# The first of eight experts on seven block products too, its normalisation moved into the units, and fill matmuls at the start of attention

## The chip, the cores and the metric

One core of a Trainium2 chip runs the whole program. The metric is device time in microseconds; lower is better. The engines are TensorE (matmul, PE), VectorE (DVE), ScalarE (ACT), GpSimd (POOL) and SyncE (SP, which issues most DMAs). All operands are float32. A float32 matmul is done here as three matmuls of `float32r` type: each factor is split into a high part (a rounded copy, on ScalarE) and a low part (the difference, on VectorE or GpSimd), and high x high, high x low and low x high are added up in PSUM.

## The reference

```python
attn_out = _attn_ref(q, k, v, proj)        # 2 x 8 heads, 768 positions, 64 wide; keys of another hash bucket are masked
x = attn_out.transpose(0, 2, 1, 3).reshape(1536, 512)
h = x @ w_in                               # 512 -> 2048
x = (h * tanh(softplus(h))) @ w_out        # Mish, 2048 -> 512
logits = x @ w_gate                        # 8 experts
P = exp(logits - logits.max())
for _ in range(8):
    P /= P.sum(1, keepdims=True) + 1e-09   # rows: one token's experts
    P /= P.sum(0, keepdims=True) + 1e-09   # columns: one expert's tokens
    P *= 1536 / 8
out = sum(P[:, e:e + 1] * (maximum(x @ w1[e], 0) @ w2[e]) for e in range(8))   # 512 -> 1024 -> 512
```

## The kernel before, in words

There are three stages. In each, every engine works through its own queue in the order in which the program issues to it.

**Attention** (`attention`, lines 178 to 772). Its steps are named tasks with engines, due times and predecessors. A planner written into the kernel (`COST`, `begin` and the loop below it) puts them in an order at build time, from costs in microseconds that stand in a table; a task's body is issued when it is chosen. `warm_up` (L268) is eight matmuls on zeros. For head h, `prep_hi` and `prep_lo` split q and k into high and low parts (head 0 in two halves, the others whole), `bits_mm` and `bits_cmp` make the bits of the hash, `s_mm` and `s_max` the row maxima, `st_mm`, `st_exp`, `split_hi`, `split_lo` and `av_mm` the rest. `clear` zeroes buffers on GpSimd once `proj_parts` (VectorE) is through. `decode` and `weight_hi`/`weight_lo` turn the first feed-forward weights, which come as 64-bit floats, into high and low parts.

**Feed-forward blocks** (lines 775 to 1098). The tokens are three blocks of 512 (`tb`), the hidden width is cut in chunks of 128 and the chunks in groups of four. `steps` lists (group, block, chunk): 48 steps for the Mish layer (chunks 0 to 15), then 24 for expert 0 (chunks 16 to 23, two groups). Loop n issues `up(n)` (12 matmuls into one PSUM bank, L814 to L816), `act(n)` (for Mish: ScalarE L826 and L827, VectorE L828) and `down(n - 3)` (12 matmuls into four banks, L850). After a block's last chunk `evacuate` adds the four banks to `acc` on VectorE (L863), and after the Mish layer `split` writes the high part `xh` on ScalarE (L866) and the low part `xl` on GpSimd (L867). What `at(n, f)` has put down is issued at the end of loop n. In this way the expert 0 steps carry beside them the `logits` of each block (8 matmuls, L876), eight whole rounds of `sinkhorn` (L904, VectorE), `spread` (four DMAs issued on ScalarE's queue, L922), and the eight token sums of the first token half, `make_t`: `raw_t` on VectorE (L975 to L981), a copy on ScalarE (L985) and the low part on VectorE (L986). They share the three scratch buffers of `t_p` with `act`.

**Units** (lines 1101 to 1297). Experts 1 to 7 take, for each half of the tokens (768) and each pair of hidden chunks, one unit. `product` computes the 2x2 block product with seven block products instead of eight (`PRODUCTS`, 42 matmuls of 384 columns, L1133), for which sums of token blocks (T1 to T4) and of weight blocks (S1 to S4, `unit_s` on GpSimd) are needed. The seven use two PSUM banks: 1, 3, 5 and 7 the one, 2, 4 and 6 the other, and `post` reads a bank between two of them. After product 1 ScalarE copies it to `p1` (L1160), product 3 is added into the same bank; after product 2 VectorE makes `u` from the other bank (L1153), product 4 is added into that. `rounded` and `rest` (L1141, L1146) split the hidden values, and `second` has the 36 matmuls of 512 columns with the second weight (L1200). `gather` adds the result, times `prob`, to `acc` (L1212). For the units to come, `unit_a`, `unit_s` and `unit_w` (ScalarE high, GpSimd low: L998, L1015 `s_lo`, L1022 `w_lo`) are issued by `job(u, s, f)` after product s, or after a quarter of the second products for s = 7 to 10. `scale_first` (L926) multiplies `acc` by expert 0's probability in units 0 to 3.

Of the kernel before, what the change touches and what calls it, by code (L numbers as in the profile page):

```python
# [16 lines left out]
P = 128  # L17
# [5 lines left out]
E = 8  # L23
# [16 lines left out]
WARM = 8  # L40
DELTA = 0.012
# [19 lines left out]
def lsh_attention_moe_kernel(  # L61
# [23 lines left out]
    cst = const.tile([P, 7 + 64], F32, name="cst")[:, 0:7]  # L85
# [13 lines left out]
    NW = N64 + NF  # L99
    NU = 2 * (E - 1) * NF // 2  # L100

    def unit(u):
        g, x = divmod(u, NU // 2)
        return g, 1 + x // (NF // 2), x % (NF // 2)
# [6 lines left out]
    def load_next():  # L111
# [9 lines left out]
        elif n < N64 + NW:  # L121
            t = stage_p.tile([P, 1024], F32, tag="stage", name="stage")
            nc.sync.dma_start(out=t, in_=w[n - 2 * N64])
            staged[n - N64] = t
        elif n < N64 + NW + 2 * NU:
            u, j = divmod(n - N64 - NW, 2)
# [34 lines left out]
    def source(i):  # L161
        return dec[i % NDEC] if i < N64 else staged[i]
# [5 lines left out]
    def convert_lo():  # L168
        i = converted[0]
        dst = ring[i % RING]  # L170
        nc.gpsimd.tensor_sub(dst[:, 1, :], source(i), f32(dst[:, 0, :]))
        converted[0] += 1
        if i >= N64:
            staged.pop(i)
            load_next()


    def attention():
        with ExitStack() as a:
# [36 lines left out]

            raw_t, hi_t, lo_t, psb_t, bit_t = {}, {}, {}, {}, {}
# [50 lines left out]
            def warm_up():  # L268
                t = ps_t.tile([P, 512], F32, tag="t", name="warm")
                for _ in range(WARM):  # L270
                    nc.tensor.matmul(t, xh[:, 0, 0:P], xh[:, 0, 0:512], start=True, stop=True)
# [8 lines left out]
            def count_rows(c):  # L280
# [3 lines left out]
                    scalar1=idt[96:100, 97:98], scalar2=float(S), op0=ALU.mult, op1=ALU.mult,  # L284
# [14 lines left out]
            def prep_lo(h, i, e):  # L299
                c = halves(h)[i]  # L300
# [27 lines left out]
            def bits_cmp(h, i):  # L328
                c = slice(i * HALF, (i + 1) * HALF)
                t = psb_t.pop(i)  # L330
                if h and i == 0:
                    bit_t[0] = bt_p.tile([44, S], F32R, tag="bit", name="bit")
                parts = [(bit_t[0], slice(0, 44))] if h else [(sq[0][64:76], slice(0, 12)), (bk[0][64:76], slice(32, 44))]
                for dst, r in parts[::-1 if i else 1]:
# [18 lines left out]
            def vsum_fin(h):  # L353
                hi, lo = (vs_p.tile([1, 2, D], F32R, tag=n, name=n) for n in ("vsh", "vsl"))
                m = vs_t[1][0:1, 0:P].rearrange("p (a d) -> p a d", a=2)
                nc.vector.tensor_copy(hi, m)
                nc.vector.tensor_sub(lo, m, f32(hi))
# [54 lines left out]
            def rows_cp(u):  # L412
# [7 lines left out]
                nc.scalar.activation(dst, src, AF.Identity, scale=cst[0:n, 5:6], bias=cst[0:n, 6:7])  # L420
# [97 lines left out]
            def task(engines, due, f, *args, after=(), cost=None, lag=0.01, ring=None, frees=None):  # L518
# [5 lines left out]
                    av_out=0.47, load_table=1.5, prep_hi=0.83, prep_move=0.83, rows_cp=0.25, st_exp=0.49,  # L524
# [4 lines left out]
                    prep_lo=0.96, s_max=0.95, cols=0.39, split_hi=0.31, split_v=0.35, vsum_red=1.53, vsum_fin=0.55,  # L529
# [3 lines left out]
                    clear=0.6, prep_lo=1.82, split_lo=1.0, split_v=0.73, norm=1.0, decode=1.3, weight_lo=2.35,  # L533
# [20 lines left out]
            task("A", -99, load_table, after=[nm(clear_start)])  # L554
            for j in range(4):
# [5 lines left out]
            for i in range(NS):  # L561
                for n, kind in enumerate(("sq", "bk", "one")):
                    e = "D" if (kind, i) in FAST else "P"
                    task(e, -8.5 + 3 * i + n / 4, clear, kind, i, after=[nm(clear, "bk", i)] * (n == 2) + [nm(proj_parts)] * (i > 0))
            for i in range(2):
                for kind in ("vt", "vh", "vl"):
                    task("P", -3 + 2 * i, clear, kind, i, after=[nm(proj_parts)])


            for h in range(NH):  # L570
# [6 lines left out]
                     after=[nm(prep_lo, hin, i) for i in range(len(halves(hin)))] if hin is not None else [])  # L577
                his = [nm(prep_hi, h, i) for i in range(len(halves(h)))]
                los = [nm(prep_lo, h, i) for i in range(len(halves(h)))]
                for i in range(len(halves(h))):  # L580
                    task("A", due - 14.0 if h else -50, prep_hi, h, i, cost=None if h else 0.45,
                         after=[nm(load_qk, h), *moved] + [nm(bits_mm, h - 1, j) for j in range(2) if h])
                    task("PD" if h else "D", due - 14.0 + 1 if h else -50, prep_lo, h, i, cost=None if h else 0.6, after=[his[i], *moved])
# [755 lines left out]
```

## Time and profile before

| | us |
|---|---|
| median of 3 runs (lowest, highest) | 1542.56 (1542.52, 1546.52) |
| the profiled execution's own time | 1542.95 |
| its span, first to last instruction | 1541.2 |
| TensorE matmul busy | 1523.3 (99%) |
| VectorE, ScalarE, GpSimd busy | 875.9, 681.3, 871.8 |

In a timeline or chain row the first number is the start in us from the span's beginning, the second the duration; "L850" is the line, "x12" means that many instructions in one row, and a bracket tells how long the engine was idle before and what ended that. Matmuls overlap in the pipeline, so two starts tell more than one duration. A VectorE or GpSimd duration includes time in which the started instruction is held up.

### The profile page before, as it was taken

Reading aid. Unit: us, or ns where it says so; the run is one execution under the profiler, and the core shown is the slowest. Engines: PE = TensorE matmul, PEld = TensorE weight load, DVE = VectorE, ACT = ScalarE, POOL = GpSimd, SP = SyncE. Lnnn points to the kernel's source line nnn. Section 1 sums busy time; section 2 is a strip of 40 time slices with the busy share of each in tenths; the row PEclk is TensorE's granted clock in tenths of the full one; section 3 lists DMA queues with packets and bytes.
Section 4 is the critical chain, followed back from the end, with each engine's and each line's share of the span. In section 5 each row is a group of like instructions: output and inputs, shape, how many; then the busy total and the mean of one; then the engine's idle time right before and its main releaser. Section 6 shows DMA issues by size and latency. Waiting matters only on the chain.

```text
span 1541.2 us, 20182 instructions
## 1 busy us (share of the span) xinstructions
PE 1523.3 (99%) x7396; PEld 1337.9 (87%) x7396; DVE 875.9 (57%) x1426; ACT 681.3 (44%) x1233; POOL 871.8 (57%) x715
## 2 busy tenths in 40 slices
PE   8999999999999999999999999999999999999999
PEld 6888888888888788889999898989898989899998
DVE  7889996746663228656444444676534444445353
ACT  5778777654443232233433333334433333333331
POOL 6887777333324230256666666666666666666661
PEclk9999999999999999999999999999999999999999
DMA  7745540122221010112222222222322222222211
GB/s 178 167 118 156 145 128 25 55 69 69 69 69 55 24 32 1 29 55 69 69 68 69 69 69 69 69 69 68 110 69 67 68 65 68 65 68 68 69 56 41
DMA packets 64387, 113.50 MB, mean 74 GB/s; under 512 B 19792, under 2 KB 20792, under 8 KB 64288
## 3 DMA queue, kind: packets, MB, share of 16 engines
q1 hardware_dynamic: 62688, 112.17, 25.1%
q8 instruction: 58, 0.95, 0.3%
q14 instruction: 41, 0.34, 0.1%
q10 hardware_dynamic: 1600, 0.05, 0.0%
HBM read 89.22 MB, written 3.15 MB: 60 GB/s over the span
## 4 chain that ended last, share of the span: by engine, by line
PE 90%; DVE 4%; DMA 2%; issue 2%; POOL 1%; ACT 1%; SPq 1%; DVEq 0%; ACTq 0%; POOLq 0%
PE y L1200 29%; PE u L1133 26%; PE y L850 13%; PE h L816 4%; PE h L814 4%; PE h L815 4%; PE pav L478 4%; PE ps L376 1%; PE pst L429 1%; PE pst L428 1%; DVE mx L390 1%; SPq L306 1%; DMA vt<-in_v_dram 1%; DMA sq<-row 0%; PE lg L876 0%
## 5 line engine op out<-in xcount | busy, mean ns | idle before, releaser
L1141 ACT ACTIVATE gh<-c 128x384 fp32r<-128x384 f32 x224 | 117.9, 526 | 153.4 <-DVE c L1153 151.6
L1153 DVE TENSOR_TENSOR u<-u,p 128x384 f32<-128x384 f32 x56 | 31.2, 558 | 266.8 <-PE u L1133 262.8
L1146 DVE SCALAR_TENSOR_TENSOR gl<-c,gh 128x384 fp32r<-128x384 f32 x224 | 168.2, 813 | 0.0
L1200 PE MATMUL y<-ww,gh 128*128 128x512 f32 x672 | 163.4, 391 | 0.0
L1200 PE MATMUL y<-w,gh 128*128 128x512 f32 x672 | 162.6, 391 | 0.0
L440 POOL TENSOR_TENSOR plo<-p,ph 128x384 fp32r<-128x384 f32 x128 | 137.3, 1084 | 43.2 <-ACT ph L437 29.5
L1200 PEld LDWEIGHTS y<-w,gh 128*128 128x128 f32 x672 | 125.7, 188 | 25.2
L1200 PEld LDWEIGHTS y<-ww,gh 128*128 128x128 f32 x672 | 125.7, 188 | 25.2
L152 POOL TENSOR_TENSOR stage<-stage,sgn 128x512 f32<-128x512 f32 x32 | 43.7, 1367 | 119.4 <-DVE sgn L150 112.1
L1022 POOL TENSOR_TENSOR w<-stage,w 128x1024 fp32r<-128x1024 f32 x28 | 66.8, 2386 | 78.4 <-ACT w L1018 78.4
L434 ACT ACTIVATE p<-pst 128x384 f32<-128x384 f32 x192 | 92.7, 486 | 40.0 <-PE pst L429 30.2
L850 PE MATMUL y<-gh,w 128*128 128x512 f32 x336 | 110.3, 389 | 0.0
L1022 POOL TENSOR_TENSOR ww<-stage,ww 128x1024 fp32r<-128x1024 f32 x28 | 66.9, 2390 | 74.3 <-ACT ww L1018 74.3
L1015 POOL TENSOR_TENSOR w<-sraw,w 128x1024 fp32r<-128x1024 f32 x28 | 68.3, 2440 | 67.7 <-ACT w L1011 67.7
L390 DVE TENSOR_REDUCE mx<-ps 128x1 f32<-128x768 f32 x95 | 90.2, 949 | 17.8 <-PE ps L376 17.1
L814 PE MATMUL h<-xh,w 128*128 128x512 f32 x252 | 98.4, 390 | 0.0
L816 PE MATMUL h<-xh,w 128*128 128x512 f32 x252 | 98.1, 389 | 0.1
L815 PE MATMUL h<-xl,w 128*128 128x512 f32 x252 | 98.1, 389 | 0.0
L998 POOL TENSOR_TENSOR wa<-stage,wa 128x512 fp32r<-128x512 f32 x28 | 40.3, 1438 | 97.2 <-ACT wa L993 69.5
L1018 ACT CAST ww<-stage 128x1024 fp32r<-128x1024 f32 x28 | 29.4, 1051 | 140.9 <-PE y L1200 140.9
L828 DVE TENSOR_TENSOR gl<-t,gh 128x512 fp32r<-128x512 f32 x48 | 47.7, 994 | 77.3 <-ACT gh L827 77.3
L1018 ACT CAST w<-stage 128x1024 fp32r<-128x1024 f32 x28 | 29.4, 1050 | 135.2 <-PE y L1200 135.2
(239 smaller groups left out, 4057.7 us busy)
## 6 DMA issues: line engine op xcount, KB each, us to landing
stage<-in_w_dram SPq DMA_DIRECT2D x152, 512.0 KB
raw<-in_qk_dram SPq DMA_DIRECT2D x13, 384.0 KB
wx<-hi SPq DMA_DIRECT2D x20, 192.0 KB
vt<-in_v_dram SPq DMA_DIRECT2D x16, 192.0 KB
out_dram<-acc SPq DMA_DIRECT2D x11, 256.0 KB
zq<-hi SPq DMA_DIRECT2D x11, 192.0 KB
ak<-hi SPq DMA_DIRECT2D x11, 192.0 KB
zq<-lo SPq DMA_DIRECT2D x11, 192.0 KB
```

What stands on the lines that cost most here:

```text
L390: nc.vector.tensor_reduce(out=m[:, t, 0:1], in_=s_t[t][:, :, :HALF], axis=AX.XY, op=ALU.max, negate=True)
L434: nc.scalar.activation(p_t[u, c], st_t.pop((u, c))[:, :HALF], AF.Exp, scale=0.125)
L440: (nc.gpsimd if e == "P" else nc.vector).tensor_sub(out, in0, in1)
L814: nc.tensor.matmul(t, wt[:, 0, f], xh[:, kc, c], start=(kc == 0), stop=False)
L815: nc.tensor.matmul(t, wt[:, 0, f], xl[:, kc, c], start=False, stop=False)
L816: nc.tensor.matmul(t, wt[:, 1, f], xh[:, kc, c], start=False, stop=(kc == KC - 1))
L850: nc.tensor.matmul(yps[j], x, y, start=(head and m == 0), stop=(tail and m == 2))
L1022: nc.gpsimd.tensor_sub(y[:, 1, :], t, f32(y)[:, 0, :])
L1133: nc.tensor.matmul(bank[x], weight(u, a, m, kc), moving(u, b, mm, kc), start=(first and n == 0), stop=(n == 5), skip_group_check=not first)
L1141: nc.scalar.activation(hi, src, AF.Relu)
L1146: nc.vector.scalar_tensor_tensor(out=lo, in0=src, scalar=0.0, in1=f32(hid_u[u, c][0]), op0=ALU.max, op1=ALU.subtract)
L1200: nc.tensor.matmul(y_t[t], (hi, hi, lo)[m][:, t % 3 * P:(t % 3 + 1) * P], y, start=(k == 0 and first), stop=(k == NF // 2 - 1 and last),)
```

## The change

Expert 0 leaves the feed-forward blocks and becomes units like the others: 48 steps are left of 72, and there are 64 units instead of 56. What ran beside the expert 0 steps gets other places:

- The token sums of the first half are issued in loops 46 to 48, the last three with feed-forward work of their own block order; type 4 runs on GpSimd instead of VectorE. The first units' weights are prepared from loop 39 on.
- The logits of blocks 0 and 1 stay in loops 45 and 49; those of block 2 go into unit 0.
- A round of the normalisation is cut in two (`sinkhorn_rows`, `sinkhorn_cols`), and the 16 halves stand three to a unit behind the second products of units 1 to 5, the last one in unit 6, where `spread` follows. Its small buffers are single instead of double.
- `gather` of expert 0 writes instead of adding: the first token half unscaled (`scale_first` follows in unit 7, six operations), the second times `prob`.
- `unit_s` for unit 2 is issued after product 5 of unit 0 instead of after product 7.

In attention, `keep_warm` issues matmuls of 256 columns on zeros into the gaps that the planner expects on TensorE until `av_count` of query block 1; `hold`, a one-element GpSimd copy, keeps GpSimd's clears behind head 0's second `prep_lo`; `prep_lo` and `weight_lo` are cut in halves; head 0's `bits_cmp` is cut in separate tasks, one of them due later; the costs in the table that belong to these change, and a factor of the mask is folded into constants. The order of the whole stage comes out of the planner anew.

```diff
+FILL = 256
-    NU = 2 * (E - 1) * NF // 2
+    NU = 2 * E * NF // 2
...
+            def keep_warm(n):
+                if nm(av_count, 1) in ends:
+                    return
+                if nm(st_mm, 0, 0) in ends and len(warm) == 1:
+                    if nm(av_count, 0) in ends:
+                        return
+                    warm.append(ps_a.tile([P, 512], F32, tag="a", name="warm"))
+                for _ in range(n):
+                    nc.tensor.matmul(warm[-1][:, :FILL], xh[:, 0, 0:P], xh[:, 0, 0:FILL], start=True, stop=True)
+
+            def hold():
+                nc.gpsimd.tensor_copy(nr[0:1, 0:1], f32(lo_t[0])[0:1, S - 1:S])
...
             def prep_lo(h, i, e):
-                c = halves(h)[i]
+                c = slice(i * HALF, (i + 1) * HALF)
...
-                    prep_lo=0.96, s_max=0.95, cols=0.39, split_hi=0.31, split_v=0.35, vsum_red=1.53, vsum_fin=0.55,
+                    prep_lo=0.56, s_max=0.95, cols=0.39, split_hi=0.31, split_v=0.35, vsum_red=1.53, vsum_fin=0.55,
...
-                    clear=0.6, prep_lo=1.82, split_lo=1.0, split_v=0.73, norm=1.0, decode=1.3, weight_lo=2.35,
+                    clear=0.6, prep_lo=1.0, split_lo=1.0, split_v=0.73, norm=1.0, decode=1.3, weight_lo=1.27,
...
+            task("P", -30, hold, after=[nm(prep_lo, 0, 1)], cost=0.15)
...
-                    task("P", -3 + 2 * i, clear, kind, i, after=[nm(proj_parts)])
+                    task("P", -3 + 2 * i, clear, kind, i, after=[nm(hold)])
...
+                if e == "E" and nm(warm_up) in ends:
+                    keep_warm(int(max(0.0, real - free[e] - 0.25) / 0.12))
...
-    NST = NTB * NW
+    NST = NTB * N64
...
-    def sinkhorn():
+    def sinkhorn_rows():
...
         nc.vector.tensor_mul(pr, pr, s.unsqueeze(2).to_broadcast([Q, n, E]))
+
+    def sinkhorn_cols():
+        n = NTOK // Q
         nc.vector.tensor_reduce(out=csum[:, 0:E], in_=pr.rearrange("p t e -> p e t"), axis=AX.X, op=ALU.add)
...
-    for tb in range(NTB):
-        n0 = start_e - (NTB - 1 - tb) * FG + LAG + 2
-        at(n0, logits, tb)
-    at(n0 + 1, put("m", sinkhorn_max))
-    at(n0 + 2, lambda: sinkhorn_exp(box["m"]))
-    for it in range(8):
-        at(n0 + 3 + it, sinkhorn)
-    at(n0 + 12, spread)
+    for tb in range(NTB - 1):
+        at(NST - (NTB - 1 - tb) * FG + LAG + 2, logits, tb)
...
-    t0 = start_e + 12
-    at(t0, open_t)
+    t0 = NST - 9
+    at(t0 + 1, open_t)
...
+        e = nc.gpsimd if k == 4 else nc.vector
+        raw_t(0, k, kc, a, b, held.get(kc), e)
+        parts_t(0, k, kc, a, e)
...
-    for x in range(8):
-        at(t0 + 4 + x, make_t, (1, 2, 4, 3)[x % 4], x // 4)
+    for n, k, kc in ((2, 1, 0), (1, 2, 0), (1, 4, 0), (1, 1, 1), (0, 2, 1), (0, 4, 1), (0, 3, 0), (0, 3, 1)):
+        at(NST - n, make_t, k, kc)
...
+        if e == 0:
+            nc.vector.tensor_scalar(out=dst, in0=y_t[t], scalar1=prob[:, i, 0:1] if g else 1.0, scalar2=None, op0=ALU.mult)
+            return
...
-            job(u, 0 if u else NP1, unit_s, u + 2)
+            job(u, 0 if u else 4, unit_s, u + 2)
...
-    for i in range(NT):
-        job(i // 3, NP1 + 1 + i % 3, scale_first, i)
+    job(0, NP1 + 1, logits, NTB - 1, ps_u, "u0")
+    job(0, NP1 + 2, put("m", sinkhorn_max))
+    job(1, 0, lambda: sinkhorn_exp(box["m"]))
+    for x, y in enumerate(divmod(n, 3) for n in range(16)):
+        job(1 + y[0], NP1 + 1 + y[1], (sinkhorn_rows, sinkhorn_cols)[x % 2])
+    job(6, NP1 + 3, spread)
+    for i in range(NT // 2):
+        job(7, NP1 + 1 + i // 3, scale_first, i)
```

## Rows read from the trace of the kernel before

**Rows 1.** Busy time by stretch: PE, PEld, DVE, ACT, POOL, clock, DMA share, GB/s.
```profile
760.00:1000.00 240.00, 240.00 (x1211) 218.20 (x1211) 115.47 (x171) 91.75 (x156) 155.86 (x125) 1.00 0.22 68
```

**Rows 2.** Chain of waits in order of time: start, duration, what.
```profile
559.07 1.85 PE lg L876 x8
...
645.26 2.72 PE y L850 x12
650.70 2.72 PE y L850 x12
...
993.66 7.33 PE u L1133 x42
...
1009.19 7.33 PE u L1133 x42
```

**Rows 3.** The same chain in the first 60 us.
```profile
16.12 0.66 PE pst L429
...
17.10 0.32 PE pbits L324
...
20.30 0.27 PE pst L429
...
27.91 0.17 PE pbits L324
```

**Rows 4.** Timeline of VectorE in the expert 0 steps: the first token sum.
```profile
619.34 0.55 DVE L975 TENSOR_TENSOR t<-xh 128x384 f32<-128x384 f32 x1
...
621.53 0.56 DVE L986 TENSOR_TENSOR tw<-t,tw 128x384 fp32r<-128x384 f32 x1 [0.58 <-ACT tw L985]
```

**Rows 5.** Timelines of VectorE, ScalarE and GpSimd: evacuation of the middle token block.
```profile
517.12 2.73 DVE L863 TENSOR_TENSOR acc<-y,acc 128x512 f32<-128x512 f32 x4 [2.40 <-PE y L850]
519.76 0.68 DVE L828 TENSOR_TENSOR gl<-t,gh 128x512 fp32r<-128x512 f32 x1
...
516.43 0.60 ACT L826 ACTIVATE t<-h 128x512 f32<-128x512 f32 x1 [6.06 <-PE h L816]
517.06 0.62 ACT L827 CAST gh<-t 128x512 fp32r<-128x512 f32 x1
517.84 2.66 ACT L866 CAST xh<-acc 128x512 fp32r<-128x512 f32 x4 [0.16 <-DVE acc L863]
...
518.54 5.54 POOL L867 TENSOR_TENSOR xl<-acc,xh 128x512 fp32r<-128x512 f32 x4 [18.09 <-ACT xh L866]
```

**Rows 6.** Timelines of VectorE and GpSimd around one unit.
```profile
1001.50 3.06 DVE L1146 SCALAR_TENSOR_TENSOR gl<-c,gh 128x384 fp32r<-128x384 f32 x4
...
1005.49 2.75 DVE L976 TENSOR_TENSOR tt<-xl 128x384 f32<-128x384 f32 x1
...
1011.40 0.56 DVE L1153 TENSOR_TENSOR u<-u,p 128x384 f32<-128x384 f32 x1 [2.58 <-PE u L1133]
...
1005.11 2.70 POOL L1015 TENSOR_TENSOR ws<-sraw,ws 128x1024 fp32r<-128x1024 f32 x1
1010.36 2.38 POOL L1022 TENSOR_TENSOR ww<-stage,ww 128x1024 fp32r<-128x1024 f32 x1 [2.54 <-ACT ww L1018]
```

**Rows 7.** Timeline of VectorE: one round of the normalisation.
```profile
575.88 0.53 DVE L906 TENSOR_REDUCE rsum<-pr 32x48 f32<-32x384 f32 x1
...
577.13 0.55 DVE L909 TENSOR_TENSOR pr<-pr,rsum 32x384 f32<-32x384 f32 x1
577.71 0.88 DVE L910 TENSOR_REDUCE csum<-pr 32x8 f32<-32x384 f32 x1
...
579.66 0.55 DVE L916 SCALAR_TENSOR_TENSOR pr<-i,pr 32x384 f32<-32x384 f32 x1
```

**Rows 8.** Timeline of all engines at the start.
```profile
4.26 0.74 POOL L249 MEMSET wx<- 1x768 f32 x1
...
4.43 0.59 DVE L276 TENSOR_SCALAR pj<-pj 64x6 f32<-64x6 f32 x1
```

**Rows 9.** Timeline of ScalarE's queue: the DMAs of the probabilities.
```profile
623.62 3.30 ACTq L922 DMA_DIRECT2D prob<-pr  x4
```

More of the change, by code (lines that the diff above doesn't have):

```diff
@@ L120, in load_next @@
             staged[i, j] = t
[L121 to L126, printed above, removed]
+        elif n < 2 * N64 + 2 * NU:
+            u, j = divmod(n - 2 * N64, 2)
             _, e, k = unit(u)
@@ L576, in attention @@
                 task("Q", due - 24 if h else -99, load_qk, h, lag=1.65 if h else 1.3, cost=0.6 if h else 1.2,
-                     after=[nm(prep_lo, hin, i) for i in range(len(halves(hin)))] if hin is not None else [])
+                     after=[nm(prep_lo, hin, i) for i in range(2)] if hin is not None else [])
                 his = [nm(prep_hi, h, i) for i in range(len(halves(h)))]
-                los = [nm(prep_lo, h, i) for i in range(len(halves(h)))]
+                los = [nm(prep_lo, h, i) for i in range(2)]
                 for i in range(len(halves(h))):
@@ L582, in attention @@
                          after=[nm(load_qk, h), *moved] + [nm(bits_mm, h - 1, j) for j in range(2) if h])
-                    task("PD" if h else "D", due - 14.0 + 1 if h else -50, prep_lo, h, i, cost=None if h else 0.6, after=[his[i], *moved])
                 for i in range(2):
-                    task("E", due - 10.0 + i, bits_mm, h, i, after=[los[i if h == 0 else 0], nm(proj_parts)], ring="m", frees=nm(bits_cmp, h, i))
-                    task("D", due - 10.0 + 1 + i, bits_cmp, h, i, cost=None if h else 1.3, after=[nm(bits_mm, h, i)]
-                         + ([nm(bits_move, h - 1, j) for j in range(2)] if h > 1 else [] if h else [nm(load_const, 1), nm(clear, "sq", 0), nm(clear, "bk", 0)]))
+                    task("PD" if h else "D", due - 14.0 + 1 if h else -50, prep_lo, h, i, after=[his[i if h == 0 else 0], *moved] + [los[0]] * i)
+                    task("E", due - 10.0 + i, bits_mm, h, i, after=[los[i], nm(proj_parts)], ring="m", frees=nm(bits_cmp, h, i) if h else nm(bits_cmp, 0, i, 1))
+                    for j in [()] if h else [(0,), (1,)]:
+                        late = 18 if not h and (i, *j) == (1, 1) else 0
+                        task("D", due - 10.0 + 1 + i + late, bits_cmp, h, i, *j, after=[nm(bits_mm, h, i)]
+                             + ([nm(bits_move, h - 1, j) for j in range(2)] if h > 1 else [] if h else [nm(load_const, 1), nm(clear, "sq", 0), nm(clear, "bk", 0)]))
                 for j in range(6):
@@ L646, in attention @@
                 pair = u - 4
-                read = [nm(norm, pair + (1 - h % 2) * 2, 4), nm(norm, pair + (1 - h % 2) * 2, 5)] if h > 1 else [nm(prep_lo, x, 0) for x in (1, 2)]
+                read = [nm(norm, pair + (1 - h % 2) * 2, 4), nm(norm, pair + (1 - h % 2) * 2, 5)] if h > 1 else [nm(prep_lo, x, i) for x in (1, 2) for i in range(2)]
                 for j in range(2):
@@ L687, in attention @@
                     last = 2 * (NH - 3 + i - RING_A) + 1
[L688 removed]
+                    task("A", due + 5, weight_hi, i, after=[nm(decode, i, x, 7) for x in range(2)] + ([nm(weight_lo, i - 1, 1)] if i else [])
                          + (gone(last, True) if i >= RING_A else []))
[L690 removed]
+                    for j in range(2):
+                        task("P", due + 6, weight_lo, i, j, after=[nm(weight_hi, i)] + [nm(weight_lo, i, 0)] * j)
             for n in range(NCH, NCH + NSTAGE):
@@ L819, in act @@
     def act(n):
-        g = step(n)[0]
         t = hps.pop(n)
@@ L1057, in lsh_attention_moe_kernel @@
     convert_lo()
-    for i in range(RING_A + NX + 1, NW):
+    for i in range(RING_A + NX + 1, N64):
         need = free[i - RING] + 1 if i >= RING else 0
-        if NATT <= i < N64:
+        if NATT <= i:
             nd = max(nd, free_dec.get(i - NDEC, 0))
@@ L1081, in lsh_attention_moe_kernel @@
                 decode(*t)
-        first = n >= LAG and step(n - LAG)[0] < NG and step(n - LAG)[4]
+        first = n >= LAG and step(n - LAG)[4]
         if first:
@@ L1096, in lsh_attention_moe_kernel @@
             f()
-    assert not side, side.keys()
+    assert not side and not early and not later, (side.keys(), early.keys())
     blocks.close()
```

131 lines of the change are left out of this document (57 added, 74 removed).

## The prediction

> **What bounds the kernel now.** I read the stretches first: between 760 and 1000 us TensorE is busy for all 240 of 240 us, VectorE for 115, GpSimd for 156, and the DMA engines for a 0.22 share [rows 1]. Then the chain of waits in order of time: from the end of attention on it is matmuls alone, a feed-forward step starting every 5.44 us and a unit every 15.53 us [rows 2]. So the last 1270 us are TensorE's, and a change there is worth the columns that it takes away, unless another engine's queue comes late. In attention TensorE is nearly full too, except for the first 25 us, where the chain runs over VectorE, DMA and slow matmuls [rows 3]. The engines around the two joints (the end of the feed-forward stage, the first units) I read one queue at a time, because each executes in program order: an instruction that waits holds everything behind it.
>
> **The gain that is meant.** Expert 0 costs 24 steps x 5.44 = 130.6 us now. As eight units it costs 8 x 15.53 = 124.3 [rows 2]. Three logits blocks of 1.85 us stay. Gain 6.3 us. Its weights are now read once for each token half, 1 MB per unit where a chunk was 0.5 MB, so 4 MB more; I cost that at nothing, because the other 56 units do the same with the DMA engines four fifths idle and TensorE never waiting [rows 1].
>
> **The join.** This is the step that I work out instruction by instruction. Call T the moment at which `down` of step 43 ends (the last of the middle token block). The token sums of the first token half need tokens 384 to 767, so nothing of them can start before T. From T, TensorE has `up` 47, `down` 44 to 47 (5 x 2.72) and one logits block (1.85): 15.45 us [rows 2]. Then come product 1 and 2 (2.1 us, from 7.33 us for 42 matmuls), and at T+17.55 product 3, which adds into product 1's bank and so waits for ScalarE's copy `p1` of it.
>
> That copy stands in ScalarE's queue behind the four `xh` copies of the last token block; these wait for the last four evacuations on VectorE; and those stand in VectorE's queue behind all eight token sums, because the sums are issued in loops 46 to 48 and the evacuations in loop 50. Each sum also has a ScalarE copy between its VectorE halves, where VectorE waits 0.58 us [rows 4].
>
> VectorE from T, with nobody in its way: evacuation and the low part of step 46 to T+1.3. A sum of type 1 or 3 takes 2.75 us (619.34 to 622.09), a type 2 one operation less, 2.3 [rows 4]; type 4 goes to GpSimd. The low part of step 47 waits for its Mish, now queued behind the first sum's copy on ScalarE: 0.6 of wait and 0.6 of work (Mish and copy 0.6 each [rows 5]). So 1.3 + 4 x 2.75 + 2 x 2.3 + 1.2 = T+18.1; the logits' transpose and add about 1.0, four evacuations 2.7 [rows 5]: T+21.9. The last `xh` copy ends 0.7 later and `p1` about 0.5 after that: T+23.3 against T+17.55. **Even without contention the stall is 5.8 us**: the gain is spent.
>
> And there is contention. GpSimd has the four low parts of the middle block (5.5 us together [rows 5]) and six operations of type 4 (about 1.0 each, an estimate from 1.3 for 512 columns [rows 5], three quarters of it). VectorE and GpSimd exclude one another when both read two operands from SBUF: a subtraction of 0.56 us is recorded with 2.75, from 1005.49 to the end of GpSimd's 2.70 us operation at 1007.81 and half a microsecond on; the additions that read PSUM stay at 0.56 while GpSimd works [rows 6]. They take turns, one operation each. Three low parts fall between VectorE's operations (3 x 1.2); of type 4's six, three fall partly into hand-off gaps (1.0 together), three don't (0.9 each): 7.3 us more. `p1` then ends at T+30.6: **a stall of 13.1 us**. I take this end, since rows of both kinds exist in this trace; the range keeps 5.8.
>
> The Trainium skill, SBUF — State Buffer, section "Who interferes with whom", has the pair of ports as an exclusive lock for the whole instruction, taken by a VectorE operation with two SBUF inputs against a GpSimd operation that reads SBUF. By this the trace agrees, with the 2.75 us above; without the lock the sum would be the 5.8.
>
> After 11 us without a matmul TensorE may restart slowly. Before 20 us the trace has 0.32 us between matmuls of 384 columns (the 1.2 GHz level), although from 16.12 on they followed one another densely; from 20.3 on it has 0.17 (2.4 GHz), while the granted clock is printed as 1.00 for both [rows 3]. Four microseconds at the lower level cost 2.0. From below it is nothing, since no long gap inside this trace shows a fall. I take 2.0.
>
> **The normalisation.** Each of eight rounds becomes two halves: rows 1.8 us (575.88 to 577.68) and columns 2.5 (to 580.21) [rows 7]. In the expert 0 stage they hid behind 5.44 us steps with GpSimd idle. Now three halves stand behind the second products of units 1 to 5, one in unit 6. VectorE is free there from the last `rest` (1004.56; the 42 first products that began at 993.66 end at 1000.99, and 3.57 us is counted from there) to the next unit's `u` (10.41: 1011.40) [rows 6], 6.84 us; three halves are 6.1 or 6.8. Alone they fit. But each half has a multiplication of two SBUF operands, and GpSimd's `s_lo` (2.70 us, until 6.8) and `w_lo` (2.38, from 9.37) lie in the same window [rows 6]. Rows, columns, rows: the first multiplication waits for `s_lo` to 6.7, the column half ends at 9.6 and `w_lo` follows at once, so the third half's multiplication waits until 11.95 and ends at 12.5; a small scaling that waits too makes it 13.3. `u` then ends at 13.1 to 13.9 for 10.97, and product 4, which adds into the bank that `u` reads, starts at 13.2 to 14.0 for 11.34: 1.9 to 2.7 us. Columns, rows, columns: the last multiplication waits for `w_lo` to 11.7, product 4 starts at 12.9: 1.6. Three units x 2.3 + two x 1.6 = **10.1 us**. The operations have 32 partitions, and no row has such a one beside GpSimd. The nearest is a scaling of 64x6 at 0.59 us beside a GpSimd memset that ends with it [rows 8], so size doesn't exempt; if partitions do, the cost is 0, which the range keeps.
>
> `spread`, four DMA issues on ScalarE's queue, took 3.30 us [rows 9]. In unit 6 they start at about 7.2, so `w_hi` (1.05) and `p1` end at 12.1 where product 3 of unit 7 wants them at 10.3: 1.9 us, from below 0 if issues pass beside compute. I take 1.9. The scalings of the first token half (six in unit 7, where there were three per unit) end before `w_lo`: nothing. The table load for Exp (in unit 1 behind `p1`) leaves `c11` in time: nothing. The earlier `unit_s` in unit 0 lies in a stretch in which TensorE waits for ScalarE: nothing.
>
> **Attention.** The fills keep TensorE occupied in the gaps of the first 25 us, so that the dense matmuls of 16.12 to 20.3 run at 0.17 instead of 0.32 [rows 3]: 2.0 us. `hold` moves GpSimd's clears behind the first low part, which takes away waits like the 0.59 [rows 8]: 0.5 to 1. Against that, fills can be in the way of a matmul that is ready early, and the halved `prep_lo` and `weight_lo` with other planner costs re-order the whole stage in a way that no row shows: from +2 to -4.5 us. I take -2.5, the size of the rows.
>
> **Sum.** The profiled run took 1542.95 for a span of 1541.2, 0.4 above the median of 1542.56, which is no difference. 1542.95 - 6.3 + 13.1 + 2.0 + 10.1 + 1.9 - 2.5 = **1561 us**.
>
> **Rivals.**
> - The small operations of the normalisation are not held by GpSimd, and the issues pass: 1561 - 12.0 = 1549. For it: 6.1 and 6.8 fit into 6.84, and reductions, reciprocals and transposes are more than half of a half round. Against it: the multiplications have two SBUF operands like the 2.75 us row.
> - In addition the sums meet no contention, and TensorE restarts fast: 1542.95 - 6.3 + 5.8 - 2.5 = 1540. Against it: rows 5 and 6.
> - The other side: the change does what it says. The place is `p1` of unit 0; it decides when that copy ends by T+17.55, for which VectorE would have to be through with the sums by about T+13.4, where the last block's first bank is complete; the working above has T+19.1 without contention. Then 1542.95 - 6.3 - 2.5 = 1534. For it: the stretch as a whole has work for VectorE of no more than TensorE's 15.45, if copies overlapped. Against it: the order of the queues.
> - Further trouble: GpSimd, still at the last block's low parts when unit 0 starts, is late with the weights of unit 1, and attention loses by its new order: 1570 to 1575.
>
> **How the numbers follow.** Forecast (1552 to 1568) 0.52; no loss in normalisation 0.13; contention-free sums 0.12; no stall 0.18; further trouble 0.05. 0.3% (4.6 us) is about what a measurement of this kernel can tell from no change, so same is 1538 to 1547.5. Slower: 0.52 + 0.13 + 0.05 = 0.70; same 0.12; faster 0.18. The range from 1536 to 1570 leaves out most of the no-stall case and of the last.
>
> **What would show it.** The chain of waits should leave TensorE after about 12 matmuls of the first unit and pass over VectorE's token sums, the evacuations and ScalarE's `p1`; TensorE should stand for some 11 us there, and matmuls behind it should be 0.32 us apart for a while. VectorE's 384-column operations of the sums should have a mean well over 0.56. Units 1 to 5 should take 17 to 18 us with product 4 waiting for `u`, unit 8 on 15.53. If the first unit starts within 2 us of the last feed-forward matmul and `p1` is punctual, the queue argument is wrong; if units 1 to 5 take 15.53, the exclusion doesn't reach the small operations. The feed-forward steps should begin some 2.5 us earlier.

## The result and the profile after

The changed kernel takes 1562.76 us (median of 5 runs; before beside it 1545.46): **ratio 1.0114, interval 1.0099 to 1.0128**; by the two medians it is 17.3 us slower. Forecast were 1561 and the range 1536 to 1570. The profiled execution took 1564.23 for a span of 1562.4, 21.2 more than before's 1541.2.

From the page of the changed kernel: engine totals, and two of the rows of 40 slices of 39 us (busy tenths of TensorE, tenths of its granted clock).

```profile
PE 1526.6 (98%) x7492; PEld 1352.1 (87%) x7492; DVE 910.4 (58%) x1470; ACT 695.7 (45%) x1266; POOL 949.1 (61%) x791
...
PE   8999999999999798999999999999999999999998
...
PEclk9999999999999899999999999999999999999999
```

Between attention and the last slice, 14 and 16 are the only ones in which TensorE is not full: the join, and the units with the half rounds. The stretches say how deep the holes are (columns: PE, PEld, DVE, ACT and POOL busy, granted clock, DMA share, GB/s), against 240 of 240 in the steady units, as in before [rows 1]:

```profile
505.00:547.00 42.00, 31.34 (x139) 24.18 (x137) 27.21 (x39) 13.11 (x24) 15.59 (x13) 0.89 0.01 3
547.00:565.00 18.00, 18.00 (x77) 15.55 (x78) 10.40 (x14) 7.29 (x13) 17.84 (x14) 0.87 0.25 70
...
582.00:600.00 18.00, 15.99 (x72) 14.23 (x72) 13.12 (x24) 4.71 (x9) 9.51 (x8) 0.91 0.20 59
...
760.00:1000.00 240.00, 240.00 (x1204) 217.32 (x1203) 125.52 (x174) 90.70 (x153) 156.32 (x123) 1.00 0.23 69
```

TensorE's own waits in the units (us in total, times, longest), where before had 0.2 in all:

```profile
PE u L1135 <- ACT p L1162: 10.8, 2, 9.9
PE u L1135 <- DVE u L1155: 9.3, 5, 2.6
```

**The join** in the chain of waits (start, duration). `down` of step 43 ends at 518.07, the T of the prediction.

```profile
519.43 1.56 DVE t L974
520.99 1.57 DVE t L975
...
522.59 1.54 DVE t L976
...
541.92 0.56 DVE tw L985
...
543.34 0.68 DVE acc L865
...
544.04 1.82 ACT xh L870 x4
...
546.36 0.48 ACT p L1162
...
546.88 3.25 PE u L1135 x9
```

The path is the one worked out: token sums, evacuation, four `xh` copies, `p1`, product 3. The first three operations of a sum take 1.6 us instead of the 0.55 of [rows 4], since GpSimd writes the middle block's low parts (L871) from 517.52 to 523.71. `p1` ends at T+28.8 (worked out: T+30.6), and product 3, ready at T+18.9, waits 9.86 us.

**The units.** The matmuls that had to wait (the bracket is the wait and its releaser):

```profile
546.88 0.69 PE L1135 MATMUL u<-xh,wx 128*128 128x384 f32 x1 [9.86 <-ACT p L1162]
585.38 3.81 PE L1135 MATMUL u<-tw,w 128*128 128x384 f32 x12 [2.00 <-DVE u L1155]
604.08 2.37 PE L1135 MATMUL u<-tw,ws 128*128 128x384 f32 x12 [1.33 <-DVE u L1155]
622.49 3.46 PE L1135 MATMUL u<-tw,w 128*128 128x384 f32 x12 [2.61 <-DVE u L1155]
...
674.69 0.44 PE L1135 MATMUL u<-xh,wa 128*128 128x384 f32 x1 [0.94 <-ACT p L1162]
```

Unit 0 takes some 31.3 us where matmuls and logits need 17.4, units 1 to 8 take 15.56, 19.37, 17.14, 19.97, 17.12, 17.80, 16.76 and 15.53. Behind some waits there is a second loss: twelve matmuls behind a wait take 2.37 us at 604.08, but 3.81 at 585.38 and 3.46 at 622.49, where the granted clock of the stretch falls to 0.91 and 0.90 (582 to 600 us, 619 to 636 us): they run at the lower level for a while.

What holds VectorE there, in unit 1 (timeline of GpSimd and VectorE):

```profile
576.15 2.39 POOL L1014 TENSOR_TENSOR ws<-sraw,ws 128x1024 fp32r<-128x1024 f32 x1
581.39 2.37 POOL L1021 TENSOR_TENSOR ww<-stage,ww 128x1024 fp32r<-128x1024 f32 x1 [2.86 <-ACT ww L1017]
...
576.77 2.17 DVE L913 TENSOR_TENSOR pr<-pr,rsum 32x384 f32<-32x384 f32 x1
...
582.07 1.73 DVE L911 TENSOR_SCALAR rsum<-rsum 32x48 f32<-32x48 f32 x1
```

The multiplication of rows (0.55 alone, as in [rows 7]) ends half a microsecond behind `s_lo`, and the addition of 1e-9 to 48 numbers (0.17 alone) ends with `w_lo`. In groups, 565 to 660 us (busy, mean ns):

```profile
L913 DVE TENSOR_TENSOR pr<-pr,rsum 32x384 f32<-32x384 f32 x8 | 9.3, 1157 | 0.3
L923 DVE SCALAR_TENSOR_TENSOR pr<-i,pr 32x384 f32<-32x384 f32 x7 | 7.4, 1059 | 0.2
L911 DVE TENSOR_SCALAR rsum<-rsum 32x48 f32<-32x48 f32 x8 | 5.0, 625 | 0.3
L910 DVE TENSOR_REDUCE rsum<-pr 32x48 f32<-32x384 f32 x8 | 4.3, 537 | 0.1
```

Reductions stay at their length beside GpSimd; multiplications and the addition to 48 columns don't. Small size alone doesn't decide it: the column half has an addition of the same kind to one column (32x1, L919), and all seven of these take 0.14 us, although four begin while `s_lo` or `w_lo` is under way.

**The balance** of the profiled execution: 8 units for 24 steps -6.3; attention -1.0 (the first `y` matmul of the feed-forward stage at 279.42, before 280.44); the join +13.9 (waits 10.7, matmuls at the lower level behind them 2.4, the rest what a stop costs beyond its wait, called refilling here); units 2 to 7 +14.9 (waits for `u` 9.3 and 0.26 of refilling behind each of the five, so 10.6; the lower level in units 2 and 4 3.1; `spread` 1.2); less 0.5 that the old join took. Sum 21.0, for 21.2 measured.

### The profile page after: what moved, and what is told of

Same layout as the page of the kernel before. It is cut to its first block, busy times and chain, and to the rows that moved or that the text cites. A ratio compares the mean times of both kernels' runs of the same rounds, so it can differ in the third digit from the quotient of the medians.

```text
span 1562.4 us, 20586 instructions
## 1 busy us (share of the span) xinstructions
PE 1526.6 (98%) x7492; PEld 1352.1 (87%) x7492; DVE 910.4 (58%) x1470; ACT 695.7 (45%) x1266; POOL 949.1 (61%) x791
## 4 chain that ended last, share of the span: by engine, by line
PE 85%; DVE 9%; issue 2%; POOL 1%; ACT 1%; DMA 1%; ACTq 0%; SPq 0%; DVEq 0%; POOLq 0%
PE y L1202 30%; PE u L1135 29%; PE y L855 8%; PE pav L488 4%; PE h L832 3%; PE h L830 3%; PE h L831 3%; PE ps L386 1%; PE pst L438 1%; PE pst L439 1%; DVE gl L1148 1%; DVE mx L400 1%; DVE pr L913 0%; POOL plo L450 0%; DMA sq<-row 0%
## 5 line engine op out<-in xcount | busy, mean ns | idle before, releaser
L1148 DVE SCALAR_TENSOR_TENSOR gl<-c,gh 128x384 fp32r<-128x384 f32 x256 | 194.8, 822 | 0.0
L1202 PE MATMUL y<-ww,gh 128*128 128x512 f32 x768 | 186.6, 391 | 0.0
L1202 PE MATMUL y<-w,gh 128*128 128x512 f32 x768 | 185.8, 391 | 0.0
L1202 PEld LDWEIGHTS y<-w,gh 128*128 128x128 f32 x768 | 143.7, 188 | 28.9
L1202 PEld LDWEIGHTS y<-ww,gh 128*128 128x128 f32 x768 | 143.7, 188 | 28.8
L1135 PE MATMUL u<-tw,w 128*128 128x384 f32 x480 | 96.3, 347 | 7.5 <-DVE u L1155 6.6
L997 POOL TENSOR_TENSOR wx<-stage,wx 128x512 fp32r<-128x512 f32 x32 | 45.2, 1411 | 90.8 <-ACT wx L992 90.8
L1202 PE MATMUL y<-ww,gl 128*128 128x512 f32 x384 | 98.2, 389 | 0.0
L1202 PE MATMUL y<-w,gl 128*128 128x512 f32 x384 | 97.4, 389 | 0.0
L1135 PEld LDWEIGHTS u<-tw,w 128*128 128x128 f32 x480 | 87.6, 195 | 9.3 <-DVE u L1155 7.9
```

Of the source, the lines that this page charges most:

```text
L997: nc.gpsimd.tensor_sub(a[:, 1, 0:512], t[:, 0, :], f32(a)[:, 0, 0:512])
L1135: nc.tensor.matmul(bank[x], weight(u, a, m, kc), moving(u, b, mm, kc), start=(first and n == 0), stop=(n == 5), skip_group_check=not first)
L1148: nc.vector.scalar_tensor_tensor(out=lo, in0=src, scalar=0.0, in1=f32(hid_u[u, c][0]), op0=ALU.max, op1=ALU.subtract)
L1202: nc.tensor.matmul(y_t[t], (hi, hi, lo)[m][:, t % 3 * P:(t % 3 + 1) * P], y, start=(k == 0 and first), stop=(k == NF // 2 - 1 and last),)
```

## Experiments

The theory has two causes. At the join, VectorE's queue (sums ahead of evacuations) makes ScalarE's `p1` late. In the units, a GpSimd instruction beside a half round holds VectorE and with it `u`. The rivals: the waits come from what is beside these (the weight work of eight more units, VectorE's mere amount of work), and move on when one cause is taken away.

Runs 1 to 6 are one execution each, and the five of the changed kernel spread from 1560.20 to 1564.46; so a difference of 2 or 3 us between their times shows little, and they are judged by their rows. Runs 7 to 12 are medians of ten, with 12 to 19 of the kernel before beside them.

**1. GpSimd's work out of the half rounds.** In units 1 to 5 `a_lo` and `s_lo` of the next unit are issued at its start, behind `w_lo`; `unit_s` later.

```diff
-            job(u, 0 if u else 4, unit_s, u + 2)
+            job(u, (3 if 2 <= u <= 6 else 0) if u else 4, unit_s, u + 2)
+            v, x = (u + 1, 0) if 1 <= u <= 5 else (u, NP1 + 1)
-            job(u, NP1 + 1, unit_a_lo, u + 2)
-            job(u, NP1 + 1, unit_s_lo, u + 2)
+            job(v, x, unit_a_lo, u + 2)
+            job(v, x, unit_s_lo, u + 2)
```

> In units 1 to 5 the low parts of the next weights (GpSimd) are issued after the next unit's first product instead of behind the second products, so that no long GpSimd operation lies beside the half rounds; VectorE's work is the same. Theory (the half rounds are held by GpSimd's operations): the multiplication of a row half, 1.16 us on average after the change, comes back to 0.55 to 0.7; units 2 to 6, which took 17.1 to 19.4 us, take 15.5 to 16.3, and the time falls by 11 to 15 us. Rival (three half rounds are too long for VectorE's free window in any case): the units stay above 17 us and the time falls by less than 3.

1560.06 us, 2.7 less than the changed kernel's median: a miss, and by its time the rival's case. Units 2 to 7 took 15.54, 17.12, 20.51, 15.54, 17.12 and 19.64 us, together 12.2 over six steady units instead of 14.9. The rows tell why it is a miss and the mechanism yet stands. In units 1 and 4 no GpSimd instruction is beside the halves, no operation is held, and units 2 and 5 have no wait: three half rounds do fit. In unit 2, `w_lo`, which I had not moved, meets the third half: its multiplication is held, the addition to one column just before it is not.

```profile
574.11 0.55 DVE L913 TENSOR_TENSOR pr<-pr,rsum 32x384 f32<-32x384 f32 x1
...
577.79 0.17 DVE L911 TENSOR_SCALAR rsum<-rsum 32x48 f32<-32x48 f32 x1
...
595.84 0.14 DVE L919 TENSOR_SCALAR r<-r 32x1 f32<-32x1 f32 x1
...
596.43 1.75 DVE L923 SCALAR_TENSOR_TENSOR pr<-i,pr 32x384 f32<-32x384 f32 x1
...
595.39 2.38 POOL L1021 TENSOR_TENSOR w<-stage,w 128x1024 fp32r<-128x1024 f32 x1 [4.67 <-ACT w L1017]
```

The 19.64 of unit 7 is the price of the move: in unit 6 `unit_s`, behind the moved low parts, lies beside `rest`, which takes 4.37 us instead of 3.05; the last half and `spread` come 1.3 later, the wait for `p1` is 2.26 instead of 0.94, and a stretch at the lower level follows it.

**2 and 3. The queue at the join.** Once the last block's four evacuations are issued behind products 2 and 4 of unit 0 (two each), with `split` at once, and once the sums are made from `acc` (one subtraction, for types 1 to 3 in two pieces, instead of two or three operations).

```diff
+    job(0, 1, last_evac, 2, False)
+    job(0, 3, last_evac, 2, True)
```

> The last token block's four evacuations and splits are issued in unit 0, two after product 2 and two after product 4, instead of ahead of unit 0. Theory (the copy of product 1 stands in ScalarE's queue behind the four high parts of the last block, these behind VectorE's evacuations, these behind the sums): the copy now follows the last sum's copy directly, product 3 starts 3.5 to 4.5 us earlier than after the change, the time falls by 3 to 5 us. Rival (product 3 waits for the sums themselves or for the banks of the last block): the wait stays at 9 to 10 us, no gain.

```diff
     def make_t(k, kc):
-        raw_t(0, k, kc, a, b, held.get(kc), e)
+        x1 = lambda j, c: acc[:, 0, j, c]
+        x2 = lambda j, c: acc[:, 0, j, HALF:TB] if c.start == 0 else acc[:, 1, j, 0:S - TB]
+        ...
+            e.tensor_sub(a[:, c], p, q)
```

> The token sums are taken from the unsplit values, which the accumulator still holds: one subtraction in two pieces (128 and 256 columns) for types 1 to 3 instead of three or two operations, and one instead of two for type 4 on GpSimd; they don't wait for the low parts on GpSimd. Theory (VectorE's queue of sums and its turns with GpSimd set the join): VectorE saves 4 x 1 us of work and 3 to 5 us of turns, the wait of product 3 falls from 9.9 to 2 to 5 us, the time by 6 to 9. Rival (the evacuations and ScalarE's handovers set it): the wait falls by less than 3.

The wait for `p1` in the first and in the second:

```profile
PE u L1152 <- ACT p L1179: 6.3, 2, 5.3
```

```profile
PE u L1142 <- ACT p L1169: 3.8, 2, 2.9
```

9.9 becomes 5.3 and 2.9, while the waits for `u` stay (9.6 and 9.3): two causes, and each takes only its own share away. The wait in run 2 fell by 4.6, for 3.5 to 4.5 expected; in run 3 it ended between the expected 2 and 5. Times 1560.78 and 1552.79. The first is 2.0 below the changed kernel's median where 3 to 5 were expected; of the second's 10.0, some 2.7 lie ahead of unit 0.

**4. No fills.** `keep_warm` returns at once.

> The changed kernel without the fill matmuls; all else, the planner's order too, is the same. Theory (the fills are worth about 1 us by the clock level of the first dense matmuls, and the rest of attention's expected gain was never there): the feed-forward steps begin 0.5 to 2 us later. Rival (the fills are in the way, and the gain is hold's and the planner's): they begin at the same time or earlier.

1564.52, and the feed-forward stage begins at 279.53, where the changed kernel's began at 279.42: by this pair the rival's case, and the fills are worth nothing. Run 7 shows why this pair misleads.

**5. One half round** (15 of the 16 are left out, so this part of the normalisation isn't computed).

```diff
-    for x, y in enumerate(divmod(n, 3) for n in range(16)):
+    for x, y in enumerate(divmod(n, 3) for n in range(1)):
```

> Leaves out 15 of the 16 half rounds of the normalisation (only the first one is left); spread, gather and everything else stay. Theory (the half rounds beside GpSimd's weight work hold up VectorE's sum u and with it product 4): units 2 to 6, which took 19.37, 17.13, 18.92, 18.19 and 17.79 us, take 15.5 each with no wait for u, so 13.8 us less than the changed kernel, of which 10.1 are the waits and 3.7 the half-level stretches behind two of them; the join keeps its wait of about 10.7. Rival (the waits for u come from the weight work of eight more units, or from the loads, and the half rounds only stand beside them): units 2 to 6 stay above 16.5, the time falls by less than 5. The length of attention varies by about 2 from run to run, so units are read by their own starts.

1548.2, 14.6 less than the median of the changed kernel. (The lengths that the expectation gives for units 4 and 5, 18.92 and 18.19, are misread: the trace has 19.97 and 17.12, with the same sum.) Every unit from the first on starts 15.54 us behind the one before, without any wait for `u`; the join waits its 9.9 as before.

```profile
563.30 7.36 PE u L1135 x42
...
578.86 7.34 PE u L1135 x42
```

Eight units' weight work and loads thus cost nothing without the half rounds; these cost all of it, the stretches at the lower level and the wait at `spread` included. This run also takes VectorE's work away; that the work alone isn't the cause is shown by units 1 and 4 of run 1.

**6. Fills in the standstill.** 84 matmuls of 256 columns between products 2 and 3 of unit 0.

```diff
+    job(0, 1, occupy, 84)
```

> The changed kernel with 84 matmuls of 256 columns (about 9 us at the higher level) into an idle PSUM bank between products 2 and 3 of the first unit, in the place of the standstill; nothing reads them. Theory (the matmuls behind the standstill run at 0.32 instead of 0.17 us because TensorE stood idle): products 3 to 7 of unit 0 take about 5.3 us instead of 7.7 and start no later, since the wait for p1 ends on ScalarE: 2.4 us less. Rival (something else slows these 30 matmuls, such as the operands being written at the time): they take 7.7 again and the time is that of the changed kernel.

In the chain of waits:

```profile
535.06 10.06 PE y L1246 x84
545.11 5.30 PE u L1135 x30
```

Products 3 to 7 take 5.30 instead of 7.71 us, as expected, and `p1` is no later. The whole took 1561.24, only 1.5 below the median: unit 6, which in the changed kernel took 17.80 with a wait of 2.00, here took 19.36 with one of 2.01. A stop of 2 us is followed by a stretch at the lower level in one execution and not in another.

**7. Before with the new attention**, nothing else of the change.

> The kernel before with the attention stage of the changed kernel (fills, hold, halved low parts, new planner costs) and nothing else of the change. Prediction's term: 2.5 us less than before, so a ratio of 0.9984. Rival from the trace of the changed kernel, whose feed-forward stage began 1.0 us earlier: 0.9994; and since five profiles of that same stage lie between 276.9 and 279.7, any of 0 to 3.7 less can be. If the ratio is 1.0000 or above, the term is wrong in sign.

**Ratio 0.9975, interval 0.9965 to 0.9985**: 1540.18 for 1544.05, -3.9 us. My -2.5 (0.9984) lies inside the interval; the -1.0 that the profile of the changed kernel had shown does not. The stretch from 14 to 20 us differs; first the changed kernel, then this one, then the one without fills:

```profile
14.00:20.00 6.00, 5.31 (x22) 4.89 (x22) 4.69 (x10) 1.52 (x4) 0.32 (x2) 0.72 0.86 181
```

```profile
14.00:20.00 6.00, 4.85 (x26) 3.86 (x26) 5.68 (x11) 2.58 (x7) 1.20 (x3) 1.00 0.85 178
```

```profile
14.00:20.00 6.00, 5.98 (x20) 5.19 (x19) 4.46 (x6) 2.14 (x6) 0.74 (x2) 0.59 0.86 175
```

With fills the `pbits` matmuls are 0.18 us apart at a granted clock of 1.00 here, and in nine of the other eleven profiles of this attention with fills; in two (the changed kernel, run 2) they are 0.32 apart at 0.72, as without fills. The ten at the higher level begin the feed-forward stage at 277.3 on average (276.4 to 278.3), the three others at 279.2: 1.9 us, about the 2.0 of the prediction, and the profile of the changed kernel is one in which the fills did not bring the higher level. For run 4 the place of the loss is another one. Without fills its first dense matmuls begin at 14.42 us, 1.7 before those of the changed kernel, and at 20 us it is as far as run 7 (its tenth `pst` matmul starts at 19.96, that of run 7 at 20.02). It falls behind between 20 and 30 us, where the changed kernel and run 7 have a granted clock of 1.00 and run 4 has this:

```profile
20.00:30.00 10.00, 7.99 (x33) 6.38 (x32) 7.17 (x15) 5.00 (x11) 5.37 (x6) 0.83 0.58 130
```

Run 4 is a single profile, and run 7 carries `hold` and the new order besides the fills, so the fills' own share of the 3.9 is not shown.

**8. Both causes taken away**: 1, 2 and 3 together, `w_hi` and `w_lo` of units 2 to 6 behind `p1`, and `spread` issued on SyncE.

```diff
-        job(u, -1 if u else NP1, unit_w_lo, u + 1)
+        job(u, 0 if 2 <= u <= 6 else -1 if u else NP1, unit_w_lo, u + 1)
...
-            nc.scalar.dma_start(out=prob[a * Q:(a + 1) * Q], ...)
+            nc.sync.dma_start(out=prob[a * Q:(a + 1) * Q], ...)
```

> The changed kernel with both causes taken away: token sums made from the unsplit rows (a VectorE operation or two less each), the last four evacuations behind the first products' sums, GpSimd's low parts a_lo and s_lo of the next unit at its start and w_lo behind p1 (out of the stretch of the half rounds), and the four issues of spread on SyncE. Theory (queues at the join, exclusion in the half rounds): wait at the join under 3 us instead of 10.7, units 2 to 7 at most 16 each; 1543 - 6.3 - 1.0 + 2 + 3 = 1540.5, a ratio of 0.998. Rival (the waits move on to the next late engine, since VectorE's work at the join and behind the second products remains): still over 5 us at the join and over 6 in the units, 1550 or more.

1547.82 (ratio 1.0026, 1.0016 to 1.0035). The join is cured: 1.3 us of waits in unit 0, which takes 19.3. The wait at `spread` is gone. But the waits for `u` are still 8.8. GpSimd, which used to stand waiting for `w_lo`, now found `a_lo` and `s_lo` at the head of its queue and began them as soon as their data were there, in the very stretch out of which I had moved them. The first half's addition was held by `s_lo`, and so the third half's met `w_lo` at 567.95:

```profile
561.15 2.71 POOL L1022 TENSOR_TENSOR ws<-sraw,ws 128x1024 fp32r<-128x1024 f32 x1
...
562.10 1.80 DVE L919 TENSOR_SCALAR rsum<-rsum 32x48 f32<-32x48 f32 x1
...
568.11 2.22 DVE L919 TENSOR_SCALAR rsum<-rsum 32x48 f32<-32x48 f32 x1
```

**9 and 10.** `w_lo` again first in the queue, and the halves as 3, 3, 3, 3, 2, 2; then the same with `w_hi` and `w_lo` behind `p1`, and the others behind them.

```diff
-    for x, y in enumerate(divmod(n, 3) for n in range(16)):
+    for x, y in enumerate((u, n) for u, m in enumerate((3, 3, 3, 3, 2, 2)) for n in range(m)):
```

> As the kernel with both causes taken away, but w_hi and w_lo back at the unit's start, ahead of a_lo and s_lo in GpSimd's queue (there they had gone ahead of w_lo and ran beside the half rounds), and the halves as 3, 3, 3, 3, 2, 2 in units 1 to 6. Theory (only a GpSimd instruction that runs beside a half round costs): behind the second products only w_lo is left, 9 us after their start; it catches the third half of a unit, 0 to 2 us in units 2 to 5, nothing in units 6 and 7; join wait under 2. Before's 1544.05, less 6.3 for the units and 3.9 for attention, and 2 and 4 to 7 more: 1540 to 1543. Rival (VectorE's own work behind the second products is too much, whoever is beside it): units 2 to 5 over 18 us each, 1547 or more.

**1540.70, ratio 0.9975 (0.9966 to 0.9985)**: faster than both kernels, and as fast as before with the new attention. Two waits for `u` are left (1.3 and 3.1), both behind a third half. The longer one follows the unit in which the first results also go out over VectorE, so that `w_lo` is met by the small addition:

```profile
598.95 2.38 POOL L1029 TENSOR_TENSOR ww<-stage,ww 128x1024 fp32r<-128x1024 f32 x1 [6.47 <-ACT ww L1025]
...
599.30 2.06 DVE L919 TENSOR_SCALAR rsum<-rsum 32x48 f32<-32x48 f32 x1
```

> The kernel of the run before, with w_hi of units 2 to 6 behind p1 on ScalarE, so that w_lo, and the low parts queued behind it, start some 1.6 us later. Theory: no GpSimd instruction beside the third half, units 2 to 7 within 1 us of 15.53, 1536 to 1540. Rival (the low parts, starting later, now run into the rest operations behind the first products, and the half rounds start later by as much): the same as the run before, or longer by 1 to 2 per unit.

1545.04 (1.0002): the rival. The low parts and `unit_s`, later by the same amount, run beside the four `rest` operations, which take 4.95 us instead of 1.96 where GpSimd is away (run 1, unit 1); the half rounds start later, and the third meets `w_lo` all the same:

```profile
574.27 4.95 DVE L1172 SCALAR_TENSOR_TENSOR gl<-c,gh 128x384 fp32r<-128x384 f32 x4
...
585.47 2.21 DVE L931 SCALAR_TENSOR_TENSOR pr<-i,pr 32x384 f32<-32x384 f32 x1
...
584.92 2.35 POOL L1029 TENSOR_TENSOR w<-stage,w 128x1024 fp32r<-128x1024 f32 x1 [5.10 <-ACT w L1025]
```

**11 and 12.** Run 9 with the halves as 3, 2, 2, 3, 3, 3; then with unit 6's low parts moved as in units 1 to 5.

> The kernel with w_lo first, with the halves as 3, 2, 2, 3, 3, 3 instead of 3, 3, 3, 3, 2, 2 in units 1 to 6, so that unit 3, where the first results also go out over VectorE, has two. Theory (w_lo catches a third half, and only then): nothing in units 3 and 4 (before: waits of 1.3 and 3.1 and a half-level stretch of about 1.8 us), at most one wait of 1.3 each in units 5 to 7: 2 to 5 us less than that kernel, 1536 to 1539. Rival (those waits came from the results that go out, not from a third half): the wait in unit 4 stays, and units 5 to 7 add theirs, 1541 or more.

1542.63 (0.9987, 0.9976 to 0.9997). Units 3 and 4 lost their waits, as expected. But unit 7 took 21.2 us with a wait of 4.0: in unit 6, which the move of run 1 leaves out, GpSimd was busy beside all three halves and held operations of the first two:

```profile
643.46 2.71 POOL L1022 TENSOR_TENSOR w<-sraw,w 128x1024 fp32r<-128x1024 f32 x1
646.13 2.38 POOL L1029 TENSOR_TENSOR w<-stage,w 128x1024 fp32r<-128x1024 f32 x1
...
644.51 1.69 DVE L919 TENSOR_SCALAR rsum<-rsum 32x48 f32<-32x48 f32 x1
...
646.71 2.20 DVE L921 TENSOR_TENSOR pr<-pr,rsum 32x384 f32<-32x384 f32 x1
```

> The kernel before this (halves 3, 2, 2, 3, 3, 3), with a_lo, s_lo and unit_s put behind w_lo in unit 6 too; there they had stayed in their old place, beside the three half rounds which that unit now has, and unit 7 took 21.2 us with a wait of 4.0 for u. Theory (only a GpSimd instruction beside a half round costs): that wait falls to 1.3 at most (w_lo beside the third half) and the half-level stretch of 1.7 us with it: 3.5 to 5 us less than 1542.6, ratio 0.995 to 0.997. Rival (unit 6 is late because three halves and spread are too much for VectorE there): the wait stays above 3, the time at 1541 or more.

1542.24 (0.9984, 0.9974 to 0.9994), no gain that can be measured. That wait fell to 1.33, as expected; but GpSimd's work, moved on by one unit, then lay beside `scale_first` in unit 7, and the next `u` waited 3.17:

```profile
659.25 7.22 DVE L941 TENSOR_SCALAR acc<-acc,prob 128x512 f32<-128x512 f32 x6
...
659.88 2.57 POOL L1022 TENSOR_TENSOR ws<-sraw,ws 128x1024 fp32r<-128x1024 f32 x1
```

Here rival and theory each have a half: who is held is decided by what stands beside it, but there is too much to place. GpSimd's low parts and sums of a unit take about 9.8 us alone (2.4 + 2.0 + 2.4 + 3.0), VectorE's operations that exclude them 3.9 (1.96 for `rest`, three multiplications of 0.55, and the small ones): an estimate of 13.7 of 15.5 us in which the two may not meet.

## Why the prediction was right

**The chain at the join** went as worked out, link by link, and run 3 and run 2 took out the two links named (the sums, the evacuations behind them). The size was high: 10.7 us of waits for 13.1, since `p1` was 1.8 us earlier than worked out and TensorE reached product 3 1.4 later. Contention, 7.3 us in the working, was nearly right: what nine VectorE operations of the sums took beyond their free 0.55 comes to 6.7. The other 1.2 of the 1.8 lie in the chain without contention, worked out as 23.3 and by this difference 22.1.

**The restart at the lower level**, 2.0 taken, was 2.4; run 6 removed it by keeping TensorE occupied. Here the granted clock shows it (0.87), other than in [rows 3].

**The half rounds**: 10.1 worked out, 10.6 measured, and in the pattern of 1.9 to 2.7 behind rows, columns, rows (2.00, 2.61, 2.00) and 1.6 behind columns, rows, columns (1.33 and 0.26 of refilling, twice). By their first matmuls it is units 2 to 6 that are longer, 17.1 to 17.8 us and, where the lower level came on top, 19.4 and 20.0. Run 5 shows that the half rounds are the cause. The reason was half right: I priced the multiplications and mentioned a small scaling in passing, but the addition to 48 numbers, with one SBUF operand, is held as long. And in rows, columns, rows it was this addition in the third half that waited for `w_lo` (582.07 to 583.80), while the multiplication behind it took 0.55. The 2.61 also has the first results in it, three operations on VectorE (L1214) that the working didn't count. The Trainium skill, SBUF — State Buffer, "Who interferes with whom", says that a `tensor_scalar` can run in a mode that takes both ports, while a `tensor_reduce` never contends on trn2; the trace agrees (625 ns on average for L911, 537 and unchanged for L910), though no run shows the mode itself. I had drawn on its rule for two inputs alone.

**What the sum lacked**: the 3.1 us at the lower level in units 2 and 4. I had looked for a fall of the clock only behind the stop of 11 us; stops of 2.0 and 2.6 us were enough, though not every time.

**`spread`** cost 1.2 for 1.9: the four issues took 2.7 us for the 3.30 of [rows 9]. On SyncE it cost nothing (runs 8 and 9).

**Attention** was worth 3.9 by run 7 for my 2.5, which its interval (2.3 to 5.4) doesn't exclude. In the profiled execution it shows 1.0.

So the errors of single terms are join -1.6 without the restart's +0.4, halves +0.5, level +3.1, spread -0.7, the old join's -0.5, and attention +1.5 in the profiled execution or -1.4 by run 7. With the first they add up to +2.7, with the second to -0.2. The change worked out is +18.3 us; the medians have +17.3, the two profiled executions +21.2. That 1561 is so near to 1562.76 is in part luck: I started from 1542.95, and the median of the kernel before beside the changed one was 1545.46.

**The rivals.** That small operations aren't held (1549) fell with the rows of unit 1; that the sums meet no contention fell with L974 to L976 at 1.6 us. The other side, `p1` in time, is what the join became once the queue was changed (run 8). With it run 9 is 4.2 us faster than before, half of the 8.8 that this rival had. But 3.9 of these belong to the attention stage (run 7): the move of expert 0 itself, repaired, comes to about nothing, its 6.3 us given back as 1.1 at the join and 6.5 of waits and lower level behind third halves.

## What to carry to other kernels

Work that is hidden beside one stage is not hidden beside another: ask of each operation which instructions of another engine will stand beside it there and hold it up, and add up the time in which the two may not meet. Read from rows which small operations belong to that sum: here the addition to 48 columns did, that to one column didn't. An instruction moved later in the program runs no later when its engine stands idle; only a queue in front of it or a dependency holds it. And read a term of 2 us from several profiles: one execution of the same attention stage showed a gain of 1.0, another 3.5.

## What was not expected of the hardware

- A VectorE addition of a constant to 32x48 numbers, 0.17 us alone, took 1.73, 1.80 and 2.06 us when a GpSimd subtraction of 128x1024 was under way, up to that one's end; reductions of 32x384 beside the same stayed at 0.54, and the addition to 32x1 numbers at 0.14.
- TensorE came back at the lower level behind stops of 2.0 to 2.6 us (12 matmuls in 3.81 and 3.46 us instead of 2.37), and behind a stop of 2.00 us in the same kernel it did not (unit 6); in run 6 it did there as well.
- With matmuls on zeros in the gaps of the first 16 us, the dense matmuls behind them ran at the higher level in ten of twelve profiles, and in two they did not; in the one profile without them they did not.
